# Splitting queries and keys once per head pair, with SBUF transfers and a block-diagonal product for the last queries

## The chip, the cores and the metric

The kernel runs on one core of one Trainium2 chip. The metric is device time in microseconds of that core, as the median over runs; less is better. The engines are named as the profile names them: PE (TensorE), DVE (VectorE), ACT (ScalarE), POOL (GpSimd), SP (SyncE, which issues most of the DMAs).

## What is computed

Attention with a threshold over 8 batches, 8 heads, 576 positions and 64 dimensions per head, and then a mixing layer of width 512 on each batch's result. All in fp32.

```python
scores = scale * np.matmul(q, k.transpose(0, 1, 3, 2))
thresh = np.max(scores, axis=-1, keepdims=True) - tau
scores = np.where(scores >= thresh, scores, -1000000000.0)
attn = np.exp(scores - np.max(scores, axis=-1, keepdims=True))
attn = attn / (np.sum(attn, axis=-1, keepdims=True) + 1e-09)
x = np.matmul(attn, v)            # heads side by side: [B, 576, 512]

theta = x @ w_theta
zr, zi = x * np.cos(theta), x * np.sin(theta)
y = np.einsum('ts,bsd->btd', w_tok_r, zr) + np.einsum('ts,bsd->btd', w_tok_i, zi)
u = x + y
out = u + np.maximum(u @ w_ch, 0.0)
```

## The kernel before

**Tiling.** A head pair (two of the eight heads of a batch) is the unit of attention; there are 32 pairs. The 576 queries of a head are four blocks of 128 and a last one of 64. Units 0 to 3 of a pair are the full blocks, each done for head 0 and then for head 1 ("half units", written (i, j)); unit 4 is the last 64 queries of both heads at once. So a pair has nine half units, in the order 0, 1, 2, 3, 4.

**Products.** To keep fp32 precision, operands are split into a high part (a cast to fp32r) and the rest. For a score, the stationary operand `qq` holds the high part of 64 dimensions on partitions 0 to 63 and the rest of the same dimensions on partitions 64 to 127; the moving operands are `k1` (high part, on both halves) and `k2` (rest). That is why `load_raw` (L213) loads each head's [64 x 576] twice, into both halves of a 128-partition tile: four 144 KB loads for a pair's queries and four for its keys. Per head ACT scales the queries (L225) and casts them (L226), POOL subtracts (L228); for keys ACT casts and POOL subtracts (`split`, L100 and L109). A full half unit is four matmuls of 288 columns (L278). Unit 4 needs both heads' keys: ten matmuls, since head 1's columns are stored rotated by 64 and its second half wraps round.

**After a score.** DVE negates it and takes the maximum (L282), ACT takes the Exp (L299), DVE masks and sums (L300). PE then transposes the result (`flip`, L326; ACT copies it, L331), and multiplies with the values (`values`, L361). At a pair's end `invert` and `normalize` divide by the sums.

**The mixing layer.** When a batch's four pairs are done its mixing layer (`moe`) is cut into pieces that `fill` puts on PE between the half units of the next batch: the angle product (L402), the sines and cosines on ACT (L463, L464, with z their result), their transposes (L487; cast zh on ACT L489, rest zl on DVE L490), the token product (L504) and the channel product (L402 again). An activation table must be loaded for Sin and again for Exp; `after` sets an order only, here the table load (L459) behind DVE's absolute value of the angle.

**Order.** PE's order is written out by hand (`manual_schedule`): at each step the score of the half unit three steps ahead (`AHEAD`), then a fill, then the flip of the present one, and another fill. On the other engines a scheduler sets the order by priority. Loads are requested at fixed half units of the pair before: queries at (0, 0), keys at (1, 0), values at unit 4. Raw tiles share a pool of four buffers (`t576`) with the angle work; key tiles have six buffers, four a pair. In the first batch the weights are also loaded and decoded from a wide format, mostly on DVE.

Of the kernel before, what the change touches and what calls it, by code (L numbers as in the profile page):

```python
# [10 lines left out]
F32 = mybir.dt.float32  # L11
# [28 lines left out]
def tile_attn_moe(  # L40
# [11 lines left out]
    nc = tc.nc  # L52
    B, NP, D, _, S = qT.shape
# [60 lines left out]
    def after(ins, other):  # L114

        info = mybir.DependencyInfo(mybir.DependencyClass.NoSync, mybir.DependencyReason.DATA)
        tc.add_manual_dep(ins.ins, other.ins.name, info, reason="order")
        return ins
# [76 lines left out]
    qq_t = []  # L195
    for i in range(2):
        qq = const.tile([P, S + SP], F32R, name=f"qq{i}")
        nc.gpsimd.memset(qq[:, S:SP].bitcast(F32), 0.0)
        qq_t.append(qq)
# [10 lines left out]
    def load_raw(n, src, name, j):  # L210
# [5 lines left out]
    def prepare_q(n, heads=(0, 1)):  # L216

        if 0 in heads:
            pairs[n] = SimpleNamespace(n=n, b=n // NP, p=n % NP, keys=[], a={})
        pr = pairs[n]  # L220
        pr.qf = qq_t[n % 2]
        for j in heads:
            raw = load_raw(n, qT, f"qraw{n}", j)
            qq = pr.qf[:, SP * j : SP * j + S]
            nc.scalar.activation(out=raw, in_=raw, func=AF.Copy, scale=gate)  # L225
            nc.scalar.copy(out=qq, in_=raw)  # L226
            eng = nc.gpsimd if n else nc.vector
            eng.tensor_tensor(out=qq[64:128], in0=raw[64:128], in1=qq[64:128].bitcast(F32), op=ALU.subtract)  # L228

    def prepare_k(n, j):  # L230

        pr = pairs[n]
        raw = load_raw(n, kT, f"kraw{n}", j)
        k1 = pool.tile([P, S], F32R, tag="k", name=f"k1_{n}_{j}", bufs=6)
        k2 = pool.tile([P, S], F32R, tag="k", name=f"k2_{n}_{j}", bufs=6)
        split(nc.scalar, nc.gpsimd if n else nc.vector, k1, k2, raw)
        pr.keys.append((k1, k2))
# [11 lines left out]
    def new_unit(n, i):  # L249
        pr = pairs[n]  # L250
        if i == 0:
# [7 lines left out]
    def score(u, j):  # L259
# [3 lines left out]
        if u.i < 4:  # L263
            c = u.i * P + (0 if j == 0 else SP + 64)
            parts = [(pr.qf[:, c : c + P], j, kk, 0) for kk in pr.keys[j]]
        else:
            parts = [(pr.qf[:, 512:SP], 0, kk, 0) for kk in pr.keys[0]]
# [424 lines left out]
```

## Time and profile before

| what | us |
|---|---|
| median of 3 runs | 1160.27 |
| fastest and slowest of them | 1159.11, 1160.57 |
| span of the profiled execution | 1161.3 |

The profile shows one execution. Busy shares of the whole span mix three parts: some 130 us in which the first batch's attention goes with the decoding of the weights, seven periods of about 133 us with one batch's attention and the batch before's mixing layer, and the last batch's mixing layer alone. So a stretch is read by itself before a line of it is. In a timeline a line gives the start, the time, the line of code, the operation, and in brackets how long its engine stood idle before it and what released it. PE's matmuls are pipelined, so the distance between two starts, not the duration, is what they take.

### The profile page before, as it was taken

What the parts mean: (1) busy time and instruction counts of PE and PEld (TensorE: products, weight loads), DVE (VectorE), ACT (ScalarE), POOL (GpSimd) and SP (SyncE); (2) the same over time, 40 slices, a digit from 0 to 9 for tenths busy, and PEclk for the clock granted to TensorE, in tenths of its full rate; (3) what the DMA queues carried; (4) which work ended last, traced back from release to release, by engine and by line L of the source; (5) the groups of instructions that cost most, each with busy time, mean ns of one, the idle gap of its engine ahead of it and who ended that gap; (6) DMA issues with size and microseconds to landing.
All of it is one profiled execution on the core that took longest, in us unless ns stands there. A gap on an engine that the chain in (4) does not pass through costs nothing.

```text
span 1161.3 us, 21157 instructions
## 1 busy us (share of the span) xinstructions
PE 1054.1 (91%) x7736; PEld 923.7 (80%) x7736; DVE 833.7 (72%) x2107; ACT 764.4 (66%) x1434; POOL 369.1 (32%) x295
## 2 busy tenths in 40 slices
PE   4987888889989999899999999899989998899998
PEld 3565686778878888798878888788878988788898
DVE  7998876986767677765877667675877667676462
ACT  6656868655696667964697657865688655965350
POOL 2203125231352233522344233422335312530110
PEclk9989999989999999999999999999999999999999
DMA  7722222343332152212432142312432133310411
GB/s 254 203 84 77 63 71 62 118 141 99 108 96 62 32 165 86 80 42 77 129 115 63 31 137 84 100 52 60 144 86 83 42 101 101 98 32 1 127 60 60
DMA packets 55176, 105.26 MB, mean 91 GB/s; under 512 B 11936, under 2 KB 20128, under 8 KB 55072
## 3 DMA queue, kind: packets, MB, share of 16 engines
q1 hardware_dynamic: 45856, 70.35, 20.3%
q0 software_dynamic: 9216, 33.56, 10.1%
q8 instruction: 61, 1.00, 0.4%
q14 instruction: 43, 0.35, 0.1%
HBM read 90.24 MB, written 13.63 MB: 89 GB/s over the span
## 4 chain that ended last, share of the span: by engine, by line
PE 54%; ACT 18%; DVE 17%; DMA 5%; issue 5%; SPq 1%; ACTq 0%; DVEq 0%
PE y_ps L504 13%; PE m_ps L402 11%; PE s_ps L278 10%; PE o_ps L361 9%; PE t_ps L326 6%; DVE s_sb L300 4%; DVE sc L282 4%; ACT s_sb L299 3%; DMA qraw<-in_qT_dram 3%; ACT z L463 2%; DMA out_dram<-xT 2%; ACT L459 2%; ACT a L331 2%; ACT L468 2%; DVE th L446 2%
## 5 line engine op out<-in xcount | busy, mean ns | idle before, releaser
L300 DVE SCALAR_TENSOR_TENSOR s_sb<-sc,nm,s_sb 128x576 f32<-128x576 f32 x288 | 274.2, 952 | 107.2 <-ACT s_sb L299 103.0
L278 PE MATMUL s_ps<-k,qq 128*128 128x288 f32 (+1 forms) x1344 | 243.7, 309 | 61.6 <-DVE sc L282 41.2
L299 ACT ACTIVATE s_sb<-sc,nm 128x576 f32<-128x576 f32 x288 | 223.7, 779 | 105.7 <-DVE sc L282 104.8
L282 DVE TENSOR_SCALAR_CACHE_REDUCE sc<-s_ps 128x576 f32<-128x576 f32 x288 | 216.7, 752 | 80.9 <-PE s_ps L278 78.1
L278 PEld LDWEIGHTS s_ps<-k,qq 128*128 128x128 f32 x1344 | 194.5, 193 | 94.3 <-DVE sc L282 52.4
L331 ACT COPY a<-t_ps 128x512 f32<-128x512 f32 x256 | 148.4, 580 | 51.8 <-PE t_ps L326 51.1
L326 PE MATMUL t_ps<-ident,s_sb 128*128 128x128 f32 x1152 | 176.6, 276 | 5.3 <-DVE zl L490 5.0
L361 PE MATMUL o_ps<-a,v 128*64 128x320 f32 (+1 forms) x1280 | 170.2, 412 | 3.5 <-DVE xT L507 3.5
L504 PE MATMUL y_ps<-wt_h,zh 128*128 128x288 f32 x576 | 166.4, 307 | 4.6 <-ACT zh L489 3.8
L504 PE MATMUL y_ps<-wt_l,zh 128*128 128x288 f32 x576 | 164.2, 303 | 0.0
L326 PEld LDWEIGHTS t_ps<-ident,s_sb 128*128 128x128 f32 x1152 | 142.0, 142 | 10.2 <-DVE zl L490 7.1
L228 POOL TENSOR_TENSOR qq<-qraw,qq 64x576 fp32r<-64x576 f32 x62 | 101.8, 1642 | 140.5 <-ACT qq L226 85.9
L361 PEld LDWEIGHTS o_ps<-a,v 128*64 128x64 f32 x1280 | 88.8, 137 | 64.0 <-issue 7.2
L109 POOL TENSOR_TENSOR k<-kraw,k 128x576 fp32r<-128x576 f32 x62 | 90.9, 1466 | 145.4 <-ACT k L100 144.5
L192 POOL DMA_DIRECT2D wm<-wm_dram x64 | 36.5, 570 | 265.7 <-PE m_ps L402 234.0
L504 PEld LDWEIGHTS y_ps<-wt_h,zh 128*128 128x128 f32 x576 | 109.2, 190 | 6.7 <-ACT zh L489 4.4
L504 PEld LDWEIGHTS y_ps<-wt_l,zh 128*128 128x128 f32 x576 | 109.4, 190 | 0.0
L504 PE MATMUL y_ps<-wt_h,zl 128*128 128x288 f32 x576 | 103.5, 305 | 0.0
L402 PE MATMUL m_ps<-xh,wm 128*128 128x288 f32 x512 | 91.1, 307 | 8.8 <-ACT th L440 8.4
L402 PE MATMUL m_ps<-uh,wm 128*128 128x288 f32 x512 | 85.0, 301 | 11.9 <-ACT uh L100 11.9
L475 POOL TENSOR_TENSOR z<-z,xT 128x576 f32<-128x576 f32 x56 | 79.5, 1442 | 32.7 <-ACT z L463 22.9
L109 POOL TENSOR_TENSOR ul<-xT,uh 128x576 fp32r<-128x576 f32 x24 | 34.7, 1446 | 169.4 <-DVE uh L104 121.4
(85 smaller groups left out, 1608.5 us busy)
## 6 DMA issues: line engine op xcount, KB each, us to landing
wm<-wm_dram POOLq DMA_DIRECT2D x64, 512.0 KB, 4.2
qraw<-in_qT_dram SPq DMA_DIRECT2D x128, 144.0 KB, 3.0
kraw<-in_kT_dram SPq DMA_DIRECT2D x128, 144.0 KB, 2.9
out_dram<-xT SPq DMA_DIRECT2D x32, 288.0 KB, 4.3
v<-in_vp_dram SPq DMA_DIRECT2D x32, 256.0 KB, 2.8
wraw<-in_w_tok_dram SPq DMA_DIRECT2D x9, 576.0 KB, 4.7
wraw<-in_w_theta_dram SPq DMA_DIRECT2D x4, 512.0 KB, 5.4
wm_dram<-whi SPq DMA_DIRECT2D x8, 256.0 KB, 2.3
```

Source lines behind the costliest of these rows:

```text
L109: eng_lo.tensor_tensor(out=lo, in0=src, in1=hi.bitcast(F32), op=ALU.subtract)
L228: eng.tensor_tensor(out=qq[64:128], in0=raw[64:128], in1=qq[64:128].bitcast(F32), op=ALU.subtract)
L278: nc.tensor.matmul(ps[:, h, d0:d1], st, kk, start=(x == 0), stop=(x == len(todo) - 1))
L282: nc.vector.tensor_scalar(out=sc.rearrange("p (a b) -> p a b", a=2), in0=ps[:, :, :HS], scalar1=-1.0, scalar2=None, op0=ALU.mult, op1=ALU.min,
L299: nc.scalar.activation(out=e, in_=u.ps[j], func=AF.Exp, bias=nm[:, j : j + 1], scale=-1.0)
L300: nc.vector.scalar_tensor_tensor(out=e, in0=u.ps[j], scalar=nm[:, 2 + j : 3 + j], in1=e, op0=ALU.is_le, op1=ALU.mult, accum_out=u.pr.rows[ ...
L326: nc.tensor.transpose(out=tp[:, c * P : (c + 1) * P], in_=u.sf[:, k0 + c * P : k0 + (c + 1) * P], identity=ident)
L331: nc.scalar.copy(out=t.a[:, :, j, q0 : q0 + P], in_=tp.rearrange("p (c q) -> p c q", c=4))
L361: nc.tensor.matmul(o[64 * j : 64 * j + 64, :w], st, mv, start=(c == 0), stop=(c == 4))
L402: nc.tensor.matmul(tiles[h][:, :HS], wm[:, a, c, :], parts[c][bb][:, hs], start=(count[h] == 0), stop=(count[h] == 11))
L475: lo_eng.tensor_tensor(out=zi, in0=zi, in1=x, op=ALU.mult)
L504: nc.tensor.matmul(ps[:, :HS], z, w, start=(n == 0), stop=(n == len(work) - 1))
```

## The change

The layout of queries and keys changes, and with it the order of the units.

- `load_raw` loads a pair's raw queries in one transfer of 128 partitions (head 0 on 0 to 63, head 1 on 64 to 127), and its keys in another. They are scaled, cast and subtracted once for both heads.
- New transfers within SBUF (`move`, on SP's queue) then build what the products need: `qq` (high part and rest of one head, four moves of 64 x 512), the key tiles (each head's part on both halves of the partitions, in `spread_k`: four moves for head 0, eight for head 1, whose columns are turned by 64 on the way), and `tails`.
- `tails` are two 128 x 128 tiles with the last 64 queries of head 0 in one corner and of head 1 in the other, zeros elsewhere. With the split keys of both heads, `kk`, as they are, unit 4 is three products of two halves: six matmuls.
- Unit 4 comes first in a pair; groups, sums and the token weights' rows and columns are reordered to match, and the output is put back by the host.
- Key tiles have four buffers (one pair) where they had six. Queries for the next pair are requested at unit 4, keys at (0, 1), the key moves at (2, 0) and (2, 1).
- The Sin table load now waits on DVE's absolute value.

```diff
     def load_raw(n, src, name):
         raw = temp(name)
-        for r in (slice(0, 64), slice(64, P)):
-            nc.sync.dma_start(raw[r], src[n // NP, n % NP, :, j])
+        nc.sync.dma_start(raw, src[n // NP, n % NP].rearrange("j d s -> (j d) s"))
         return raw
...
+    def prepare_q(n):
+        pr = pairs[n] = SimpleNamespace(n=n, b=n // NP, p=n % NP, keys=[], a={}, tails=tails)
+        raw = load_raw(n, qT, f"qraw{n}")
+        hi = temp(f"qh{n}", F32R)
+        lo = raw.bitcast(F32R)
+        nc.scalar.activation(out=raw, in_=raw, func=AF.Copy, scale=gate)
+        nc.scalar.copy(out=hi, in_=raw)
+        eng = nc.gpsimd if n else nc.vector
+        eng.tensor_tensor(out=lo, in0=raw, in1=hi.bitcast(F32), op=ALU.subtract)
+        for t, x in zip(tails, (hi, lo)):
+            for j in range(2):
+                r = slice(64 * j, 64 * j + 64)
+                move(t[r, r], x[r, 512:])
+        pr.qq = []
+        for j in range(2):
+            qq = pool.tile([P, 512], F32R, tag="qq", name=f"qq{n}_{j}", bufs=4)
+            for x, y in ((0, hi), (64, lo)):
+                move(qq[x : x + 64], y[64 * j : 64 * j + 64, :512])
+            pr.qq.append(qq)
...
+    def spread_k(n, j):
+        pr = pairs[n]
+        for x in range(2):
+            t = pool.tile([P, S], F32R, tag="k", name=f"k{x}_{n}_{j}", bufs=4)
+            src = pr.kk[x][64 * j : 64 * j + 64]
+            for r in (slice(0, 64), slice(64, P)):
+                if j == 0:
+                    move(t[r], src)
+                else:
+                    move(t[r, 64:], src[:, :512])
+                    move(t[r, :64], src[:, 512:])
+            pr.keys.append(t)
...
         else:
-            parts = [(pr.qf[:, 512:SP], 0, kk, 0) for kk in pr.keys[0]]
-            parts += [(pr.qf[:, S : S + P], 1, kk, 64) for kk in pr.keys[1]]
+            (qh, ql), (kh, kl) = pr.tails, pr.kk
+            parts = [(qh, kh), (qh, kl), (ql, kh)]
...
-            ahead_of = after(nc.scalar.preload_act_table(AF.Sin), ab)
+            ahead_of = after(nc.scalar.preload_act_table(AF.Sin), ab, wait=True)
...
-    halfs = [(n, i, j) for n in range(B * NP) for i in range(5) for j in range(2 if i < 4 else 1)]
+    halfs = [(n, i, j) for n in range(B * NP) for i in (4, 0, 1, 2, 3) for j in range(2 if i < 4 else 1)]
...
             if n + 1 < B * NP:
-                if (i, j) == (0, 0):
+                if i == 4:
                     prepare_q(n + 1)
-                if (i, j) == (1, 0):
-                    for jj in range(2):
-                        prepare_k(n + 1, jj)
-                if i == 4:
+                if (i, j) == (0, 1):
+                    prepare_k(n + 1)
+                if (i, j) == (1, 1):
                     load_v(n + 1)
+                if i == 2:
+                    spread_k(n + 1, j)
```

On PE, pair 16's unit 4 (a row is the line, the operation, its output and inputs, and the shape; `k1_16_j` and `k2_16_j` are the high part and the rest of head j's keys). Before:

```order
L278 MATMUL s_ps_6654<-k1_16_0_6148,qq0_83 128x288
L278 MATMUL s_ps_6654<-k2_16_0_6149,qq0_83 128x288
L278 MATMUL s_ps_6654<-k1_16_1_6155,qq0_83 128x288
L278 MATMUL s_ps_6654<-k2_16_1_6156,qq0_83 128x288
L278 MATMUL s_ps_6654<-k1_16_0_6148,qq0_83 128x288
L278 MATMUL s_ps_6654<-k2_16_0_6149,qq0_83 128x288
L278 MATMUL s_ps_6654<-k1_16_1_6155,qq0_83 128x224
L278 MATMUL s_ps_6654<-k1_16_1_6155,qq0_83 128x64
L278 MATMUL s_ps_6654<-k2_16_1_6156,qq0_83 128x224
L278 MATMUL s_ps_6654<-k2_16_1_6156,qq0_83 128x64
```

The same unit, now at the pair's start, where `kh16` and `kl16` are both heads' split keys and `tail_h`, `tail_l` the block-diagonal queries:

```order
L293 MATMUL s_ps_6436<-kh16_6292,tail_h_83 128x288
L293 MATMUL s_ps_6436<-kl16_6293,tail_h_83 128x288
L293 MATMUL s_ps_6436<-kh16_6292,tail_l_85 128x288
L293 MATMUL s_ps_6436<-kh16_6292,tail_h_83 128x288
L293 MATMUL s_ps_6436<-kl16_6293,tail_h_83 128x288
L293 MATMUL s_ps_6436<-kh16_6292,tail_l_85 128x288
```

Ten matmuls became six of 288 columns, on tiles that no key move writes.

On ACT, a block of sines beside pair 14, before (L299 is the Exp, L331 and L344 flip copies, L489 the cast zh):

```order
L459 ACT_TABLE_LOAD
L463 ACTIVATE z_5311<-z_5311,small_74 128x576
L464 ACTIVATE z_5311<-th_5090 128x576
L464 ACTIVATE z_5313<-th_5166 128x576
L331 COPY a0_5197<-t_ps_5382 128x4x128
L344 COPY a50_5198<-t5_ps_5388 128x128
L299 ACT_TABLE_LOAD
L299 ACTIVATE s_sb_5364<-sc_5371,nm_5365 128x576
L463 ACT_TABLE_LOAD
L463 ACTIVATE z_5313<-z_5313,small_74 128x576
L468 ACT_TABLE_LOAD
L489 CAST zh_5410<-z_ps_5412 128x128
```

The same block after:

```order
L316 ACTIVATE s_sb_5513<-sc_5520,nm_5514 128x576
L476 ACT_TABLE_LOAD
L480 ACTIVATE z_5437<-z_5437,small_74 128x576
L481 ACTIVATE z_5437<-th_5207 128x576
L480 ACTIVATE z_5439<-z_5439,small_74 128x576
L481 ACTIVATE z_5439<-th_5288 128x576
L485 ACT_TABLE_LOAD
L316 ACTIVATE s_sb_5513<-sc_5560,nm_5514 128x576
```

The four sines stand together, and the two loads around an Exp between them are gone; this is so in the seven blocks that had them.

On SP, the program's start, before (the number in `qraw0`, `kraw0` is the pair):

```order
L80 DMA small_74<-in_tau_dram 128x1
L213 DMA qraw0_93<-in_qT_dram 64x576 x2
L213 DMA kraw0_99<-in_kT_dram 64x576 x2
L213 DMA qraw0_106<-in_qT_dram 64x576 x2
L213 DMA kraw0_112<-in_kT_dram 64x576 x2
L132 DMA wraw_171<-in_w_theta_dram 128x1024
```

And after:

```order
L80 DMA small_74<-in_tau_dram 128x1
L216 DMA qraw0_93<-in_qT_dram 128x576
L133 DMA wraw_205<-in_w_theta_dram 128x1024
L133 DMA wraw_187<-in_w_theta_dram 128x1024
L133 DMA wraw_320<-in_w_theta_dram 128x1024
L133 DMA wraw_300<-in_w_theta_dram 128x1024
L133 DMA wraw_450<-in_w_tok_dram 128x1152
L216 DMA kraw0_109<-in_kT_dram 128x576
L216 DMA qraw1_209<-in_qT_dram 128x576
L212 DMA tail_h_83<-qh0_95 64x64 x2
L212 DMA tail_l_85<-qraw0_93 64x64 x2
L212 DMA qq0_0_103<-qh0_95 64x512
```

Five weight loads moved ahead of the first pair's keys and of its moves; two more (of `w_tok`) stand between those of the queries and those of the keys.

On SP, the key moves of pair 22 after, a third pair of its batch (`kh22`, `kl22` are the split keys, `k0_22_j` and `k1_22_j` the tiles of head j):

```order
L216 DMA kraw22_8847<-in_kT_dram 128x576
L212 DMA k0_22_0_8979<-kh22_8849 64x576 x2
L212 DMA k1_22_0_8982<-kl22_8850 64x576 x2
L212 DMA k0_22_1_9021<-kh22_8849 64x512
L212 DMA k0_22_1_9021<-kh22_8849 64x64
L212 DMA k0_22_1_9021<-kh22_8849 64x512
L212 DMA k0_22_1_9021<-kh22_8849 64x64
L212 DMA k1_22_1_9026<-kl22_8850 64x512
```

Twelve new transfers follow the load in the queue, of which the four for head 0 come first; before there were none.

## Rows read from the trace of the kernel before

**Rows 1.** The page's first part: busy us, share of the span, instructions.

```profile
PE 1054.1 (91%) x7736; PEld 923.7 (80%) x7736; DVE 833.7 (72%) x2107; ACT 764.4 (66%) x1434; POOL 369.1 (32%) x295
```

**Rows 2.** Three stretches: length, busy us by engine, clock, DMA share, GB/s.

```profile
0.00:30.00 30.00, 13.32 (x42) 10.02 (x43) 21.36 (x51) 18.53 (x28) 6.53 (x14) 1.00 0.80 256
30.00:100.00 70.00, 60.65 (x324) 42.95 (x322) 67.81 (x160) 45.89 (x92) 15.53 (x11) 0.93 0.46 131
681.00:815.00 134.00, 125.25 (x956) 111.60 (x957) 95.28 (x251) 92.96 (x175) 48.30 (x37) 1.00 0.30 85
```

**Rows 3.** PE's timeline near 706 us: start, us, line, in brackets idle time before.

```profile
706.32 1.42 PE L278 MATMUL s_ps<-k,qq 128*128 128x288 f32 x10
707.57 0.78 PE L402 MATMUL m_ps<-xh,wm 128*128 128x288 f32 x4
...
709.80 0.69 PE L278 MATMUL s_ps<-k,qq 128*128 128x288 f32 x4
710.33 0.69 PE L402 MATMUL m_ps<-xh,wm 128*128 128x288 f32 x4
```

**Rows 4.** PE's timeline, waits on ACT, DVE and POOL from 730 to 751.

```profile
730.77 0.66 PE L326 MATMUL t_ps<-ident,s_sb 128*128 128x128 f32 x4 [0.92 <-DVE zl L490]
...
733.15 0.80 PE L278 MATMUL s_ps<-k,qq 128*128 128x288 f32 x4 [0.49 <-DVE sc L282]
...
745.47 0.63 PE L487 MATMUL z_ps<-ident,z 128*128 128x128 f32 x4 [0.79 <-DVE zl L490]
...
747.11 0.67 PE L278 MATMUL s_ps<-k,qq 128*128 128x288 f32 x3 [0.48 <-POOL k L109]
...
750.51 0.78 PE L278 MATMUL s_ps<-k,qq 128*128 128x288 f32 x4 [0.70 <-DVE rows L366]
```

**Rows 5.** ACT's timeline around raw queries and sines, same batch.

```profile
728.74 0.78 ACT L225 ACTIVATE qraw<-qraw,small 128x576 f32<-128x576 f32 x1 [3.06 <-DMA qraw<-in_qT_dram]
...
739.26 1.28 ACT L299 ACT_TABLE_LOAD   x1
...
741.35 1.28 ACT L463 ACT_TABLE_LOAD   x1
...
743.44 1.28 ACT L468 ACT_TABLE_LOAD   x1
744.73 0.27 ACT L489 CAST zh<-z_ps 128x128 fp32r<-128x128 f32 x1
```

**Rows 6.** Groups by line and form: count, busy us, mean ns, idle before.

```profile
L300 DVE SCALAR_TENSOR_TENSOR s_sb<-sc,nm,s_sb 128x576 f32<-128x576 f32 x288 | 274.2, 952 | 107.2 <-ACT s_sb L299 103.0
...
L225 ACT ACTIVATE qraw<-qraw,small 128x576 f32<-128x576 f32 x64 | 49.8, 779 | 24.9 <-DMA qraw<-in_qT_dram 21.8 <-DVE sc L282 3.0
L100 ACT CAST k<-kraw 128x576 fp32r<-128x576 f32 x64 | 43.2, 675 | 29.1 <-PE s_ps L278 26.9 <-DMA kraw<-in_kT_dram 2.0
L226 ACT CAST qq<-qraw 128x576 fp32r<-128x576 f32 x64 | 43.2, 675 | 0.5
```

**Rows 7.** DVE's and POOL's timelines, same batch.

```profile
747.64 1.42 POOL L109 TENSOR_TENSOR k<-kraw,k 128x576 fp32r<-128x576 f32 x1 [0.59 <-ACT k L100]
...
748.28 1.40 DVE L300 SCALAR_TENSOR_TENSOR s_sb<-sc,nm,s_sb 128x576 f32<-128x576 f32 x1 [0.59 <-ACT s_sb L299]
```

**Rows 8.** DMA issues: count, KB each, median us from issue to landing.

```profile
qraw<-in_qT_dram SPq DMA_DIRECT2D x128, 144.0 KB, 3.0
...
out_dram<-xT SPq DMA_DIRECT2D x32, 288.0 KB, 4.3
...
wraw<-in_w_theta_dram SPq DMA_DIRECT2D x4, 512.0 KB, 5.4
```

**Rows 9.** SP's queue: one issue of two half loads; SP's waits by releaser.

```profile
726.93 1.19 SPq L213 DMA_DIRECT2D qraw<-in_qT_dram  x2
...
SPq L213 <- DVE th L446: 217.8, 14, 29.7
```

**Rows 10.** PE's timeline, the first score.

```profile
8.58 1.79 PE L278 MATMUL s_ps<-k,qq 128*128 128x288 f32 x4 [8.58 <-DVE qq L228]
```

More of the change, by code (lines that the diff above doesn't have):

```diff
@@ L112, in temp, with after @@
         return pool.tile([P, S], dt, tag="t576", name=name, bufs=4)
-    def after(ins, other):
-        info = mybir.DependencyInfo(mybir.DependencyClass.NoSync, mybir.DependencyReason.DATA)
+    def after(ins, other, wait=False):
+        kind = mybir.DependencyClass.Sync if wait else mybir.DependencyClass.NoSync
+        info = mybir.DependencyInfo(kind, mybir.DependencyReason.DATA)
         tc.add_manual_dep(ins.ins, other.ins.name, info, reason="order")
@@ L193, in get_wm @@
         return t
[L195 to L199, printed above, removed]
+    tails = []
+    for x in ("h", "l"):
+        t = const.tile([P, P], F32R, name="tail_" + x)
+        nc.gpsimd.memset(t.bitcast(F32), 0.0)
+        tails.append(t)
     v5_t = []
@@ L208, in tile_attn_moe, with move, load_raw @@
     pairs = {}
-    def load_raw(n, src, name, j):
+    def move(out, in_):
+        nc.sync.dma_start(out.bitcast(F32), in_.bitcast(F32))
+    def load_raw(n, src, name):
         raw = temp(name)
-        for r in (slice(0, 64), slice(64, P)):
-            nc.sync.dma_start(raw[r], src[n // NP, n % NP, :, j])
-        return raw
-    def prepare_q(n, heads=(0, 1)):
-        if 0 in heads:
-            pairs[n] = SimpleNamespace(n=n, b=n // NP, p=n % NP, keys=[], a={})
-        pr = pairs[n]
[L221 to L228, printed above, removed]
@@ new lines, in prepare_k @@
+    def prepare_k(n):
+        pr = pairs[n]
+        raw = load_raw(n, kT, f"kraw{n}")
+        pr.kk = [pool.tile([P, S], F32R, tag="kk", name=f"{x}{n}", bufs=2) for x in ("kh", "kl")]
+        split(nc.scalar, nc.gpsimd if n else nc.vector, *pr.kk, raw)
+    def spread_k(n, j):
+        pr = pairs[n]
+        for x in range(2):
[8 more added lines that the diff above has]
+            pr.keys.append(t)
@@ L347, in flip_last @@
                 r = slice(64 * j, 64 * j + 64)
-                nc.scalar.copy(out=t.a5[r, 256:320], in_=tp[r, r])
+                nc.scalar.copy(out=t.a5[r, :64], in_=tp[r, r])
     def values(pr, g):
@@ L361, in values @@
                 nc.tensor.matmul(o[64 * j : 64 * j + 64, :w], st, mv, start=(c == 0), stop=(c == 4))
[L362 removed]
+        nc.scalar.copy(out=xT[pr.n][:, 320 * g : 320 * g + w], in_=o[:, :w])
     def invert(pr):
@@ L665 @@
     last = vv[:, :, :, 512:].reshape(B, H // 2, 128, 1, D)
-    wr = _np.asarray(inputs["moe_w_tok_r"]).T
-    wi = _np.asarray(inputs["moe_w_tok_i"]).T
+    wr = _np.asarray(inputs["moe_w_tok_r"]).T[order][:, order]
+    wi = _np.asarray(inputs["moe_w_tok_i"]).T[order][:, order]
     feeds = {
@@ L690 @@
     got = r.results[0]["out_0_dram"]
-    return _np.ascontiguousarray(got.transpose(0, 2, 1))
+    out = _np.empty((B, S, H * D), got.dtype)
+    out[:, order] = got.transpose(0, 2, 1)
+    return out
```

58 lines of the change are left out of this document (23 added, 35 removed).

## The prediction

> **What bounds the kernel now.** I read the page's busy shares first: PE is busy for 91% of the span, DVE for 72%, ACT for 66% [rows 1]. That is a mean, so next I read the stretches [rows 2]. From 30 to 100 us DVE is the engine without room (67.81 of 70 us: the weights are decoded there beside batch 0's attention), and PE runs at a clock of 0.93. In a later batch, 681 to 815 us, PE has 125.25 of 134 us at clock 1.00, and DVE 95.28, ACT 92.96 and POOL 48.30. So in seven of the eight batches the time is PE's own work plus the 134.00 − 125.25 = 8.75 us in which PE, whose instructions run in a fixed order, waits for an input. Anything taken from ACT, POOL or the DMA queues counts only if one of those waits ends on it. The reader is to see in PE's own rows which waits these are [rows 4].
>
> **PE's own work.** A pair's ten-matmul unit is at 706.32 and the next line starts at 707.57: 1.25 us. An ordinary unit's four matmuls take 710.33 − 709.80 = 0.53 us, 0.133 each [rows 3]. Six cost 0.80, so a pair gains 0.45 us. It counts in the 28 pairs of batches 1 to 7; in batch 0 DVE hides it. 28 × 0.45 = **−12.6 us**. This term is sure, unless PE waits for the product's inputs: the block-diagonal queries and the keys of both heads. These need only the load, the split and the 16 KB moves, and are issued more than half a pair ahead.
>
> **ACT and POOL.** Two heads' scaling and two casts become one of each on 128 partitions: ACT loses 32 × (779 + 675 + 675) ns = 68 us [rows 6]. In ACT's order the 14 sine tables that are loaded again inside a block go too, 14 × 1.28 = 18 us [rows 5]. Of 764 us that is 11%, but off PE's path; it is worth what it takes from PE's 8.75 us. I looked behind each wait:
> - 730.77 (0.92 us) and 733.15 (0.49): ACT had just been given the two heads' raw queries, late (3.06 us of waiting, then 0.78 and 0.67 us of work for each head [rows 5, 6]); the cast zh and the Exp that PE waited for stood behind them. One of two sets remains: half, 0.70 us.
> - 745.47 (0.79): the cast zh at 744.73 stood behind the loads at 739.26, 741.35 and 743.44. Two of the three go, 2.6 us: all of it.
> - 747.11 (0.48) and 750.51 (0.70): the first waits for POOL's subtraction for a key tile. The second stands behind a DVE mask that took 1.40 us beside the next one on POOL [rows 7]; its kind takes 0.95 on the mean [rows 6]. In the changed order the key split comes a turn and a half earlier, once: all of it, 1.18.
>
> Together 0.70 + 0.79 + 1.18 = 2.67 us a batch; 7 × 2.67 = **−18.7 us**. The low end is nothing (another wait ends just behind), the high one all five, 3.38 × 7 = −23.7. The rest of the 8.75 us isn't touched and stays.
>
> **The added wait.** The sine table's load now waits for DVE's absolute value, with Exps, flip copies and zh casts queued behind it on ACT, and PE behind those. The sine itself needed that value already, and the rows show no idle time there but a block in pieces [rows 5]. Scores run three half units ahead, so I cost it at nothing; if that cover is gone, it gives back the 0.79 of 745.47, which is inside the bounds above.
>
> **The moves.** SP's queue gets 20 moves a pair and loses 6 loads of 8. At 0.60 us an issue [rows 9] 25 issues are 15 of a pair's 33 us, so SP isn't full. What matters is when the last key move lands. Keys now have buffers for one pair only, so head 1's eight moves can't start before the last score of the pair has read the old keys, and must land before the next pair's (0, 1) score. By the rows of the changed order and 0.133 us a matmul, PE has 9.0 us of work between those two points (9.0 to 9.4 in the four pairs of a batch); for head 0 it is about the same with half the moves. No SBUF-to-SBUF transfer stands in this trace. The nearest row for issuing one is a 64-partition load, 1.19 / 2 = 0.60 us [rows 9]; for landing, the 144 KB load, 3.0 us, and at the bad end the slowest load, 5.4 [rows 8]. Eight issues and one landing behind the 0.53 us of the last score: 0.53 + 4.8 + 3.0 = 8.3, inside 9.0 by 0.7 us. I take 3.0, since the bytes and partitions are those of that row. Once a batch an output of 288 KB stands in the same queue; with its landing, 4.3, the sum is 9.6, 0.6 us late: 7 × 0.6 = **+4 us**. Third pairs have a longer chain: their raw load waits for a buffer that DVE's angle work frees, a wait SP has 14 times, up to 29.7 us [rows 9]; raw queries, split, moves and raw keys then follow one another. That leaves 0 to 4 us late each batch, so the ends of this term are 0 and +28.
>
> The Trainium skill speaks against this part: "DMA: Bandwidth & Descriptors", section Rules for kernel authors, says that two transfers to disjoint partition halves serialize and that one 128-partition transfer should be used. By it head 1's moves wouldn't overlap, and the last could land as at the bad end above. No run here shows two such moves; this trace's pairs of half loads do land at 3.0 us.
>
> **The start.** Before, the first score runs at 8.58 us [rows 10]. Now one load of queries is followed on SP by five weight loads, 2.6 MB, before the first moves. At the 256 GB/s of the first 30 us [rows 2], 3.2 MB take 12.6 us, and a landing of 3.0 puts the first score at 15 to 16: 7 us late. The per-head keys come behind two more weight loads, so the upper end is twice that, +14. Against this stand DVE's 30.00 − 21.36 = 8.6 idle us [rows 2]: weights that come sooner can be decoded there, and what isn't left for 30 to 100 us is won back; half of it, −4, is the low end. I take **+5 us**, the middle.
>
> **The sum.** Against the profiled execution, 1161.3: −12.6 − 18.7 + 4 + 5 = −22.3, so 1139.0. The median of the runs lies 1.0 below the span: **1138**.
>
> **Rivals.** *Keys late in every pair.* If moves land like the slowest load, 0.53 + 4.8 + 5.4 = 10.7 us against 9.0: 1.7 us of PE waiting at (0, 1), 28 × 1.7 = 48 us. 1161.3 − 12.6 − 18.7 + 5 + 48 − 1.0 = **1182**, slower. It decides from 26.3 / 28 = 0.94 us a pair, that is when head 1's last move lands more than 9.9 us after the previous pair's last score. For it: eight serial issues, and a buffer for one pair only. Against it: 0.7 us of margin at this trace's own landings, and DMA busy 30% of a batch. Chance 0.18.
>
> *ACT and POOL were cover only.* The PE waits stay, each ending on the next thing: 1161.3 − 12.6 + 4 + 5 − 1.0 = **1157**. For it: the wait at 750.51 stands only 3.4 us behind the one at 747.11, so one that goes may leave the next. Against it: 86 us gone from ACT, spread over all batches. Chance 0.13.
>
> *The start costs all of +14:* 1138 + 9 = **1147**. For it: eight loads ahead of the key moves. Against it: DVE's idle time. Chance 0.10.
>
> The forecast with its own spread, 1121 to 1150, has the other 0.59.
>
> **The numbers.** The range reaches below to all five waits gone and the best start, 1161.3 − 12.6 − 23.7 − 4 − 1.0 = 1120; I put 1119. Above, it takes in the late start and the covered ACT; of the first rival it takes the mild third (the third pairs alone, +28 in place of +4, give 1162), and ends at 1166. Left out are about 0.14 above and 0.04 below. A measurement of this kernel tells 0.2% from no change, here 1158.0 to 1162.6. Faster: the forecast 0.58, the late start 0.10, half of the covered case 0.07, together 0.75. Same: the other half and a mild lateness, 0.08. Slower: 0.17.
>
> **What would show it.** Score units of six matmuls near 0.80 us; no table load inside a sine block; ACT about 86 us less busy; no PE wait of the kinds at 730.77, 745.47 and 747.11. The first score at about 15 us, and the second batch's first Exp no more than 5 us later than before. A PE wait at the (0, 0) or (0, 1) score that ends on a key move, in most pairs and of a microsecond or more, would make the forecast wrong; in third pairs alone it would cost what I allowed. So would a first batch longer by over 14 us.

## The result and the profile after

The changed kernel takes 1149.63 us (median of 4 runs, 1148.71 to 1151.60), the kernel before 1160.42 beside it; the ratio is 0.9889, interval 0.9866 to 0.9911. The forecast of 1138 had the way right and double the size: 10.8 us were gained, not 22. Two more measurements beside the kernel before, on other chips, gave 0.9942 (0.9924 to 0.9960) and 0.9916 (0.9889 to 0.9943). The mean of the three is 0.9916, about 10 us, and chips differ by more than one interval; so below a run is set against the kernel before measured beside it on the same chip. Where the changed kernel wasn't measured beside it too, the comparison with that kernel is uncertain by the spread of these three, some 3 us either way.

The profiled execution spans 1146.9 us, 14.4 less than before. The page's first part shows that all engines have less to do [rows 1]:

```profile
PE 1033.3 (90%) x7608; PEld 907.0 (79%) x7608; DVE 821.2 (72%) x2105; ACT 682.8 (60%) x1324; POOL 271.2 (24%) x233
```

ACT lost 81.6 us where I had counted 86, POOL 98. The groups by line and form show how: half as many scalings and casts at the same price as before [rows 6], and 16 table loads each way, none inside a block.

```profile
L225 ACT ACTIVATE qraw<-qraw,small 128x576 f32<-128x576 f32 x32 | 24.9, 779 | 29.1 <-DMA qraw<-in_qT_dram 28.0 <-issue 1.0
L100 ACT CAST kh<-kraw 128x576 fp32r<-128x576 f32 x32 | 21.8, 682 | 13.8 <-DMA kraw<-in_kT_dram 13.7
L226 ACT CAST qh<-qraw 128x576 fp32r<-128x576 f32 x32 | 21.7, 678 | 0.8 <-DVE kl L109 0.8
L476 ACT ACT_TABLE_LOAD x16 | 20.5, 1283 | 6.1 <-DVE z L472 6.0
L485 ACT ACT_TABLE_LOAD x16 | 20.5, 1283 | 0.3
```

On PE's timeline a pair's first unit now runs from 703.41 to 704.31, where its ten matmuls took 1.25 us [rows 3]:

```profile
703.41 0.40 PE L293 MATMUL s_ps<-kh,tail_h 128*128 128x288 f32 x1
703.65 0.30 PE L293 MATMUL s_ps<-kl,tail_h 128*128 128x288 f32 x1
...
704.18 0.29 PE L293 MATMUL s_ps<-kh,tail_l 128*128 128x288 f32 x1
704.31 0.70 PE L419 MATMUL m_ps<-xh,wm 128*128 128x288 f32 x4
```

That is 0.90 us, 0.10 more than six times 0.133, since the first of them takes 0.24. The units of the other pairs take 0.89 to 0.91. A pair gains 0.35 us, 28 pairs 9.8.

**Where the time went.** The first Exp of each batch, read from ACT's timeline, cuts the span into stretches (us). Batches are counted from 0; "b1" and "b2 to b6" are the time from a batch's first Exp to the next one's, and "rest" is the last batch with its mixing layer:

| kernel | first Exp | first Exp of b1 | b1 | b2 to b6 | rest | span |
|---|---|---|---|---|---|---|
| before | 11.2 | 138.3 | 143.3 | 667.0 | 212.7 | 1161.3 |
| after | 19.2 | 139.9 | 136.5 | 661.4 | 209.1 | 1146.9 |
| after, second measurement | 19.1 | 139.4 | 141.7 | 663.2 | 209.8 | 1154.1 |
| after, third | 19.5 | 141.1 | 137.1 | 662.2 | 209.7 | 1150.1 |

The five steady batches gain only 4 to 6 us, about 1 a batch, where PE's own work alone should give 4 × 0.35 = 1.4 and the waits 2.7 more. Batch 1, which was 10 us longer than the steady ones before, gains 2 to 7 us by itself, and the rest 3 to 4.

So new waits stand where old ones went. The list of PE's waits over the five steady batches (us in total, times, the longest) has, before:

```profile
PE s_ps L278 <- DVE sc L282: 11.3, 11, 1.6
PE m_ps L402 <- ACT th L440: 6.0, 5, 1.2
```

and after:

```profile
PE s_ps L293 <- DVE sc L299: 22.2, 24, 2.2
PE z_ps L504 <- ACT th L457: 10.2, 5, 2.0
```

The kinds at 730.77, 745.47, 747.11 and 750.51 [rows 4] made up 10.4 us before, and none of them is left. But PE stands idle for 42.5 us of these batches (43.8 and 42.9 in the other two profiles), and it was 41.0 before. PE's timeline and the clock of four stretches show the longest wait that comes in every batch, behind the sines:

```profile
583.49 0.91 PE L504 MATMUL z_ps<-ident,z 128*128 128x128 f32 x4 [2.04 <-ACT th L457]
584.54 1.33 PE L419 MATMUL m_ps<-xh,wm 128*128 128x288 f32 x4
585.80 3.01 PE L378 MATMUL o_ps<-a,v 128*64 128x256 f32 x20
```

```profile
581.00:583.40 2.40, 0.45 (x5) 0.21 (x2) 0.02 (x1) 2.37 (x5) 2.40 (x3) 1.00 0.17 60
583.40:586.00 2.60, 2.37 (x10) 1.72 (x12) 2.56 (x2) 2.59 (x7) 2.24 (x2) 0.56 0.00 0
586.00:588.00 2.00, 2.00 (x16) 1.13 (x16) 2.00 (x5) 0.99 (x3) 0.00 (x0) 0.72 0.30 83
588.00:590.00 2.00, 2.00 (x19) 1.54 (x16) 0.71 (x3) 0.84 (x2) 0.00 (x0) 1.00 0.46 134
```

PE stands for 2.04 us behind ACT's eviction of the angle. In the stretch that begins with its return the granted clock is 0.56, near the lower level (1.2 GHz), and four matmuls that else take 0.78 take 1.33. From 588 on it is 1.00 again. ACT's timeline shows why the eviction was late:

```profile
577.74 1.28 ACT L476 ACT_TABLE_LOAD   x1 [0.67 <-DVE z L472]
...
581.64 1.28 ACT L485 ACT_TABLE_LOAD   x1
582.94 0.41 ACT L457 ACTIVATE th<-m_ps 128x288 f32<-128x288 f32 x1
```

The table load waits 0.67 us for DVE's absolute value: the added wait. Then load, four sines and load hold ACT until 582.94. A batch has two blocks of sines; this is the first, which was in one piece before too.

The second kind, on DVE's and PE's timelines while the queries of a third pair are being moved:

```profile
599.89 0.46 DVE L462 TENSOR_SCALAR km<-th 128x576 f32<-128x576 f32 x1 [2.51 <-DMA qq<-qh]
...
601.06 0.75 DVE L299 TENSOR_SCALAR_CACHE_REDUCE sc<-s_ps 128x576 f32<-128x576 f32 x1
...
601.87 0.81 PE L293 MATMUL s_ps<-k,qq 128*128 128x288 f32 x4 [1.84 <-DVE sc L299]
```

DVE's angle step takes a tile of the shared pool that the query moves still read. It stands 2.51 us, the copy of the scores (L299) behind it, and PE behind that. This happens once in each of six batches, 7.1 us in all on DVE. Each time the move that DVE waited for had landed 3.1 to 5.2 us after its issue, with a 512 KB weight tile (`wm`) issued shortly before it; half of all such moves land in 2.4 or less. A third kind is the raw query load behind twelve key moves in SP's queue:

```profile
808.47 0.78 ACT L225 ACTIVATE qraw<-qraw,small 128x576 f32<-128x576 f32 x1 [2.55 <-DMA qraw<-in_qT_dram]
```

An Exp stands behind it, and the next score on PE:

```profile
813.23 0.80 PE L293 MATMUL s_ps<-k,qq 128*128 128x288 f32 x4 [2.18 <-DVE sc L299]
```

What didn't happen is key tiles coming late pair after pair. Outside the first 30 us one score waits on one, at some 248 us, for 1.0 us (3.9 and 1.3 in the other two profiles). The page's list of DMA issues gives the median landing of head 0's key moves:

```profile
k<-kh SPq DMA_DIRECT2D x64, 144.0 KB, 2.5
k<-kl SPq DMA_DIRECT2D x64, 144.0 KB, 2.7
```

### The profile page after: what moved, and what is told of

It is laid out like the page before. It is cut to its first block, busy times and chain, and to the rows that moved or that the text cites. A ratio compares the mean times of both kernels' runs of the same rounds, so it can differ in the third digit from the quotient of the medians.

```text
span 1146.9 us, 21522 instructions
## 1 busy us (share of the span) xinstructions
PE 1033.3 (90%) x7608; PEld 907.0 (79%) x7608; DVE 821.2 (72%) x2105; ACT 682.8 (60%) x1324; POOL 271.2 (24%) x233
## 4 chain that ended last, share of the span: by engine, by line
PE 49%; DVE 15%; ACT 15%; DMA 9%; SPq 6%; issue 5%; ACTq 0%; DVEq 0%
PE y_ps L521 13%; PE s_ps L293 9%; PE o_ps L378 8%; PE m_ps L419 8%; SPq L212 6%; PE t_ps L343 5%; DVE s_sb L317 4%; DMA qraw<-in_qT_dram 3%; DVE sc L299 3%; ACT s_sb L316 3%; DMA kraw<-in_kT_dram 2%; ACT z L480 2%; DMA qq<-qraw 2%; DVE xl L109 2%; ACT L476 2%
## 5 line engine op out<-in xcount | busy, mean ns | idle before, releaser
L317 DVE SCALAR_TENSOR_TENSOR s_sb<-sc,nm,s_sb 128x576 f32<-128x576 f32 x288 | 264.2, 917 | 79.4 <-ACT s_sb L316 74.4
L299 DVE TENSOR_SCALAR_CACHE_REDUCE sc<-s_ps 128x576 f32<-128x576 f32 x288 | 216.6, 752 | 113.9 <-PE s_ps L293 111.4
L293 PE MATMUL s_ps<-k,qq 128*128 128x288 f32 x1024 | 195.1, 313 | 56.4 <-DVE sc L299 48.5
L293 PEld LDWEIGHTS s_ps<-k,qq 128*128 128x128 f32 x1024 | 151.9, 193 | 73.9 <-DVE sc L299 63.6
L378 PE MATMUL o_ps<-a,v 128*64 128x256 f32 (+1 forms) x1280 | 175.9, 422 | 1.1 <-ACT a L350 1.0
L228 POOL TENSOR_TENSOR qraw<-qraw,qh 128x576 fp32r<-128x576 f32 x31 | 44.3, 1429 | 212.7 <-ACT qh L226 206.8
L492 POOL TENSOR_TENSOR z<-z,xT 128x576 f32<-128x576 f32 x56 | 82.8, 1508 | 29.4 <-ACT z L480 29.4
L521 PEld LDWEIGHTS y_ps<-wt_h,zl 128*128 128x128 f32 x576 | 83.5, 189 | 0.0
L419 PEld LDWEIGHTS m_ps<-uh,wm 128*128 128x128 f32 x512 | 72.0, 188 | 13.8 <-ACT uh L100 13.3
```

The source lines that it names most:

```text
L228: eng.tensor_tensor(out=lo, in0=raw, in1=hi.bitcast(F32), op=ALU.subtract)
L293: nc.tensor.matmul(ps[:, h, :HS], st, kk[:, h * HS : (h + 1) * HS], start=(x == 0), stop=(x == len(parts) - 1))
L299: nc.vector.tensor_scalar(out=sc.rearrange("p (a b) -> p a b", a=2), in0=ps[:, :, :HS], scalar1=-1.0, scalar2=None, op0=ALU.mult, op1=ALU.min,
L317: nc.vector.scalar_tensor_tensor(out=e, in0=u.ps[j], scalar=nm[:, 2 + j : 3 + j], in1=e, op0=ALU.is_le, op1=ALU.mult, accum_out=u.pr.rows[ ...
L378: nc.tensor.matmul(o[64 * j : 64 * j + 64, :w], st, mv, start=(c == 0), stop=(c == 4))
L419: nc.tensor.matmul(tiles[h][:, :HS], wm[:, a, c, :], parts[c][bb][:, hs], start=(count[h] == 0), stop=(count[h] == 11))
```

## The experiments

The sections give the ratio to the kernel before, measured beside it, and its interval. "Lost to the clock" is, over windows of 2 us, the sum of PE's busy time × (1 − granted clock), in batches 2 to 6; the kernel before has 0.0 there, the changed kernel 6.3, 6.5 and 6.6 in its three profiles.

### Four matmuls back in

```diff
-            parts = [(qh, kh), (qh, kl), (ql, kh)]
+            parts = [(qh, kh), (qh, kl), (ql, kh), (qh, kl), (ql, kh)]
```

> The changed kernel, with ten matmuls of 288 columns in the first unit of a pair in place of six (two products are added a second time, so the last queries' scores are other numbers; the work around them is the same). Theory (the matmuls taken out are worth their own time in seven batches): 28 x 4 x 0.133 = 15 us longer, 1164 to 1165. Rival (PE's order has slack at that place, so matmuls there cost little): under 7 us longer, below 1157.

Ratio 1.0047 (1.0022 to 1.0072), median 1168.1: against the mean of the changed kernel, 0.9916, that is 0.0131, 15 us longer (12 to 18 against its three measurements), as the first theory says. Batches 2 to 6 take 671.2 us, 9 more than the changed kernel, where 20 × 4 × 0.133 is 10.6. PE's order has no slack at that place; the term for PE's own work stands. These ten matmuls are not those of the kernel before: all have 288 columns, and the unit takes 1.43 us where the old ten took 1.25, so the run puts back more (0.53 us a pair) than the change took out (0.35).

### Lighter ACT and POOL without the moves

The kernel before, with head 1 on head 0's operands from the second pair on:

```diff
-        for j in heads:
+        for j in heads if n == 0 else (0,):
...
+        if j == 1 and n > 0:
+            pr.keys.append(pr.keys[0])
+            return
...
-            c = u.i * P + (0 if j == 0 else SP + 64)
+            c = u.i * P + (0 if j == 0 or pr.n else SP + 64)
...
-            parts += [(pr.qf[:, S : S + P], 1, kk, 64) for kk in pr.keys[1]]
+            last = pr.qf[:, 512:SP] if pr.n else pr.qf[:, S : S + P]
+            parts += [(last, 1, kk, 64) for kk in pr.keys[1]]
```

> The kernel before, in which from the second pair on head 1 takes head 0's queries and keys (its results are head 0's scores with head 1's values; head 1's queries and keys are neither loaded nor split). PE's instructions are the same in number and shape; ACT is relieved of 66 us and POOL of some 96 us, as by the change, without any move and without the six-matmul unit. Recorded sum: the waits behind queries and keys go, 0.70 + 1.18 us in seven batches, 13 us shorter, 1147 where the kernel before has 1160 (ratio 0.989). Theory now (a PE wait that goes lets the next one in): under 5 us shorter, ratio 0.996 or more.

Ratio 0.9813 (0.9787 to 0.9838), median 1142.45 against 1164.26: 22 us, more than the recorded sum and four times what my theory after the result allowed. That theory falls: waits of PE that go behind queries and keys do shorten the run. The page's first part shows PE's instructions unchanged in number [rows 1] and ACT and POOL relieved about as in the changed kernel:

```profile
PE 1043.0 (91%) x7736; PEld 913.6 (80%) x7736; DVE 832.1 (73%) x2107; ACT 706.3 (62%) x1341; POOL 278.3 (24%) x233
```

The gain lies all along: the first Exp of batch 1 at 133.7 (before 138.3), batch 1 140.0, batches 2 to 6 659.7, the rest 208.2. So the relief helps the first batch too, which I had not counted: 4.6 us. The loads of head 1 are gone here as well, 4 of 8 a pair, and so are half the takers of raw tiles and of the six key buffers, so the 22 us hold whatever those cost; the run doesn't separate it.

### The waiting table load alone, and both together

```diff
-            ahead_of = after(nc.scalar.preload_act_table(AF.Sin), ab)
+            ahead_of = after(nc.scalar.preload_act_table(AF.Sin), ab, wait=True)
```

in the kernel before, and in the light kernel above (with `after` taught to wait, as in the changed kernel).

> The kernel before with the one edit that the Sin table load waits on DVE's absolute value; 14 table loads go from ACT. Recorded sum: 0.79 us in seven batches, 5 to 6 us shorter (ratio 0.995). Theory now (the block of sines in one piece holds PE for 2 us, and some batches then run 4 us at the lower clock): no gain, ratio 0.999 to 1.006, with granted clocks under 1 behind that wait in several of the batches 2 to 6, where the kernel before has none.

> Both at once: the kernel before with head 1 on head 0's queries and keys (results as in the first run of this call) and the waiting table load; all that the change takes from ACT and POOL, and nothing else of it. Recorded sum: 19 us shorter, ratio 0.984. Theory now: under 7 us shorter, ratio 0.994 or more.

Alone: ratio 1.0036 (1.0019 to 1.0053), 4 us slower. In the light kernel: 0.9855 (0.9831 to 0.9878), 5 us more than without. The wait costs, in both. In the kernel before with the wait, PE's timeline and the clock of two stretches read:

```profile
594.86 0.79 PE L403 MATMUL m_ps<-xh,wm 128*128 128x288 f32 x4 [1.37 <-ACT th L441]
595.58 4.60 PE L362 MATMUL o_ps<-a,v 128*64 128x320 f32 x20
```

```profile
596.00:598.00 2.00, 2.00 (x12) 0.89 (x10) 2.00 (x2) 1.98 (x4) 1.09 (x1) 0.51 0.00 0
598.00:600.00 2.00, 2.00 (x12) 0.76 (x8) 2.00 (x6) 0.48 (x2) 0.00 (x0) 0.64 0.39 93
```

In the kernel before, the same wait is 1.21 us, the clock behind it stays at 1.00, and the same twenty value matmuls take 2.91 us:

```profile
721.53 0.81 PE L402 MATMUL m_ps<-xh,wm 128*128 128x288 f32 x4 [1.21 <-ACT th L440]
722.27 2.91 PE L361 MATMUL o_ps<-a,v 128*64 128x320 f32 x20
```

PE's wait for this eviction is only 0.16 us longer than in the kernel before. The larger new wait stands behind the second block of sines, the one that the added wait makes one piece. On POOL's and PE's timelines:

```profile
611.97 5.56 POOL L476 TENSOR_TENSOR z<-z,xT 128x576 f32<-128x576 f32 x4 [3.23 <-issue]
617.49 3.81 POOL L109 TENSOR_TENSOR k<-kraw,k 128x576 fp32r<-128x576 f32 x2
...
619.47 0.72 PE L279 MATMUL s_ps<-k,qq 128*128 128x288 f32 x3 [1.92 <-POOL k L109]
```

The four sines come in a row, POOL's four operations on them too, and both key subtractions stand behind these. Over batches 2 to 6 PE waits 9.8 us for POOL's key tiles, where it was 1.9. Lost to the clock in these batches: 12.7 us, three stretches behind the eviction, three behind POOL's key tiles and one with another wait, of 2.98 us. The five batches take 671.4, 4.4 more. Without that loss they would be 658.7, 8 us under the kernel before, if none of the lost time was covered by other waits. So taking the loads out of the block may bring what I had counted or more, and POOL's late subtraction and the clock take more than that back. In the light kernel POOL has half the subtractions, and PE never waits for a key tile there. For both together the recorded sum (19 us, 0.984) lies inside the interval; my theory's 0.994 doesn't.

The reverse edit, in the changed kernel:

> The changed kernel, with the Sin table load ordered behind DVE's absolute value but not waiting on it, as before; the 14 loads inside the sine blocks come back. Theory (the sine blocks in one piece cost a wait of 2.0 us and some 0.5 to 2 us of slow PE clock behind it in each batch, 0.7 of it by the added wait): 0 to 7 us shorter than the changed kernel, 1143 to 1150. Rival (the recorded sum: the loads cost 0.79 us a batch of PE's time, and nothing speaks against taking them out): 5 to 6 us longer, 1155.

Ratio 0.9916 (0.9893 to 0.9940), the mean of the changed kernel's three measurements, none of which stood beside this one. On PE's timeline the wait behind the sines is 0.65 us shorter, and the twenty value matmuls behind it run at full clock:

```profile
584.66 0.63 PE L504 MATMUL z_ps<-ident,z 128*128 128x128 f32 x4 [1.39 <-ACT th L457]
585.71 0.79 PE L419 MATMUL m_ps<-xh,wm 128*128 128x288 f32 x4 [0.42 <-ACT a L348]
586.43 2.38 PE L378 MATMUL o_ps<-a,v 128*64 128x256 f32 x20
```

Nothing is lost to the clock in batches 2 to 6, and yet they take 667.3 us, no less than before: smaller waits stand in other places (0.69, 0.62 and 1.07 us at scores between 593 and 613). In the changed kernel no price of the wait is to be seen.

### Tiles of their own for the queries

```diff
-        raw = load_raw(n, qT, f"qraw{n}")
-        hi = temp(f"qh{n}", F32R)
+        raw = pool.tile([P, S], F32, tag="qraw", name=f"qraw{n}", bufs=1)
+        nc.sync.dma_start(raw, qT[n // NP, n % NP].rearrange("j d s -> (j d) s"))
+        hi = pool.tile([P, S], F32R, tag="qh", name=f"qh{n}", bufs=1)
```

> The changed kernel, with the raw queries and their high part in tiles of their own (one buffer each) and not in the shared pool of four. Theory (new waits took the place of the old): in the changed kernel DVE's angle step waits for moves that still read such a tile, 7.1 us in six batches, and the raw keys of a third pair come late for ACT, 11 us in the same batches; both go, each batch gets 1 to 2 us shorter, and the time is 6 to 12 us under the changed kernel's 1149.6: 1138 to 1144. Rival (PE's floor is reached, the next wait stands right behind): no more than 2 us less, 1147 to 1150.

Ratio 0.9979 (0.9947 to 1.0010), 4 to 10 us slower than the changed kernel; neither forecast held. DVE's waits on moves are gone, 0 where there were 6.6 us in batches 2 to 6; the time isn't. These batches take 664.0 us, and 11.2 are lost to the clock. PE's waits for the copy of the scores fell from 22.2 to 13.0 us, but 9.4 us of others came (for DVE's zl and ACT's flip copy) that the changed kernel hasn't. The profiled execution was the fastest of ten, 9 us under their median, so the trace doesn't show where the median's loss lies.

Then the same with the table load not waiting:

> The changed kernel with two edits: the raw queries and their high part in tiles of their own, and the Sin table load not waiting on DVE. Theory (of the gain of 22 us that the lighter ACT and POOL bring, some is lost to tiles that moves hold, and what the own tiles gave back in the first call was eaten by the lower clock behind the one-piece sine block): without that block both count, no slow-clock stretch in batches 2 to 6, and the time is 5 to 12 us under the changed kernel of this call. Rival (the loss is not in held tiles; late raw loads and the key chain remain, whatever holds them): within 3 us of the changed kernel of this call.

Ratio 0.9984 (0.9967 to 1.0001): also slower than the changed kernel (0.9916 beside it), and neither forecast held. Freeing the tiles brought nothing that can be seen; since new waits came with it, that doesn't show what the held tiles cost. Lost to the clock 7.3 us, three stretches of it with a wait of 2.47 us for DVE's zl, so the waiting table load isn't the only thing that lowers the clock. The first Exp of batch 1 came at 148.1, 8 us later than in the changed kernel; why I did not find. The scheduler's order on ACT and DVE is another one in both kernels.

### The first pair's keys ahead of the weights

```diff
         raw = load_raw(n, qT, f"qraw{n}")
+        if n == 0:
+            pr.kraw = load_raw(0, kT, "kraw0")
...
-        raw = load_raw(n, kT, f"kraw{n}")
+        raw = pr.kraw if n == 0 else load_raw(n, kT, f"kraw{n}")
```

> The changed kernel, with the first pair's keys loaded right behind its queries, and its key moves ahead of the later weight loads. Theory (DVE's decoding sets the first 130 us, the late first score is made up there): the first Exp comes 4 to 8 us earlier, the end no more than 3 us, 1147 to 1150. Rival (the late start is passed on): 5 to 8 us shorter, 1142 to 1145.

Ratio 0.9902 (0.9873 to 0.9932): within the changed kernel's three. The first Exp is 1.5 us earlier (17.7), the second batch's comes at 140.5. The edit moved the load, but most of the key moves still issue behind those of the queries, from 15 us on, and the start moved less than meant; so it bounds little; what can be said is that 1.5 us at the front weren't seen again at 140.

### The moves without anybody waiting for them

The light kernel, with 20 transfers a pair from a weight tile to two spare tiles, requested at the change's places:

```diff
+                if n >= 4 and (i, j) == (0, 1):
+                    qmoves()
+                if n >= 4 and i == 2:
+                    moves(j)
```

> The kernel before with head 1 on head 0's queries and keys from the second pair on (as in the second call), and from the fifth pair on 20 transfers within SBUF a pair, of the change's sizes and at its places, from a weight tile to two spare tiles that nobody reads: the moves' traffic and their place in SP's queue, without anyone waiting for them. The light kernel without them had ratio 0.981. Theory (what the moves cost is waits of engines for tiles and late loads in the chain of one pair): under 4 us more, ratio 0.981 to 0.985. Rival (traffic and queue: slower landings and later loads for everybody): 8 us or more on top, ratio 0.988 or more.

Ratio 1.0140 (1.0093 to 1.0186): 38 us over the light kernel. By the number the rival wins. But the run isn't what it was meant to be: nobody waits for these transfers and their source is ready early, and they didn't stay at their places. The trace has the first of the 540 at 50.7 us, in batch 0, the last at 545.5, in batch 3, some 40 a pair, twice the change's density; from batch 4 (563.1) on there is none. Yet batches 4 to 6 are 9 us longer than in the light kernel, batches 2 and 3 11.

Where the transfers are, SP's and ACT's timelines show a raw load among them, and ACT behind the load:

```profile
473.67 1.18 SPq L236 DMA_DIRECT2D qraw<-in_qT_dram  x2
...
477.94 0.78 ACT L248 ACTIVATE qraw<-qraw,small 128x576 f32<-128x576 f32 x1 [3.93 <-DMA qraw<-in_qT_dram]
```

And in all five steady batches two subtractions stand in a row on DVE's timeline ahead of the copy of the scores, which stood between them in the light kernel. In batch 4, and PE's wait in batch 6:

```profile
577.88 3.24 DVE L109 TENSOR_TENSOR xl<-xT,xh 128x576 fp32r<-128x576 f32 x2
581.04 0.74 DVE L309 TENSOR_SCALAR_CACHE_REDUCE sc<-s_ps 128x576 f32<-128x576 f32 x1
...
849.99 0.80 PE L305 MATMUL s_ps<-k,qq 128*128 128x288 f32 x4 [3.42 <-DVE sc L309]
```

PE waits 3.42 us there, where the light kernel waits 1.55, and the clock falls behind it in four of the five (6.5 us lost). That is 5 × 1.87 + 6.5 = 16 of the 20 us by which these batches are longer (679.9 against 659.7). In three of them no transfer to a spare tile runs, so it is the scheduler's order, moved by the added instructions, and no price of a transfer. The first two batches are 14 us longer, with transfers and another order at once; what is whose there stays open. So the run shows that an order can cost 16 us, and not what the change's moves cost.

### Raw loads from another queue

```diff
-        nc.sync.dma_start(raw, src[n // NP, n % NP].rearrange("j d s -> (j d) s"))
+        (nc.gpsimd if n else nc.sync).dma_start(raw, src[n // NP, n % NP].rearrange("j d s -> (j d) s"))
```

> The changed kernel with the raw query and key loads issued by POOL, from the second pair on, and not by SP, whose queue keeps the moves, the values and the outputs. ACT's order stays nearly the same. Theory (the moves cost by standing ahead of the raw loads in one queue, and ACT, in order, stands at a raw tile with the Exp behind it): ACT's waits for raw tiles in batches 2 to 6 fall from 29 us to under 14, and the time is 5 to 10 us under the changed kernel: ratio 0.982 to 0.987 where the changed kernel had 0.989 to 0.994. Rival (traffic, or the chain from tile to tile, whichever queue issues): those waits stay above 20 us, ratio 0.989 to 0.996.

Ratio 1.0003 (0.9973 to 1.0034): the gain is gone, and neither forecast held. ACT's waits for raw tiles in batches 2 to 6 fell to 15.4 us, from 28.8 to 29.1 in the three profiles of the changed kernel; over the whole run they are

```profile
ACT qraw L225 <- DMA qraw<-in_qT_dram: 20.7, 8, 4.5
...
ACT kh L100 <- DMA kraw<-in_kT_dram: 8.3, 8, 1.5
```

in place of 28.0 and 13.7. But batches 2 to 6 take 663.4 us, no less, with 8.0 lost to the clock; and the first batch and the second are longer (first Exp of batch 1 at 144.9, its period 144.8). POOL now stands at loads whose tiles aren't free, 53.3 us behind query moves and 14.4 us once behind the decoding of the weights, with its subtractions and weight tiles queued behind it. Two of POOL's lines of waits:

```profile
POOL kraw L216 <- DMA qq<-qraw: 53.3, 9, 6.7
...
POOL kraw L216 <- DVE mag L140: 14.4, 1, 14.4
```

The loads' waits moved from ACT to POOL; the run doesn't show what late raw loads on ACT cost.

### The changed kernel again

> The changed kernel itself, on the same chip as the other runs of this call, so that they can be set beside it: ratio 0.989 as at first, within its interval of 0.002.

> The changed kernel, on the same chip as the other runs of this call, to set them beside it: ratio 0.989 to 0.994, as in the two measurements so far.

0.9942 and 0.9916, as above. The first is outside what I expected: the same kernel on another chip differs by 0.005. The second lies inside.

## Why the prediction was right or wrong

**PE's own work: right, the size somewhat too large.** Recorded −12.6; the unit takes 0.90 us and not 0.80, so −9.8, and four matmuls put back cost 15 us, their own time.

**The waits behind ACT and POOL: right in kind, and rather more.** Recorded −18.7, of it 13 behind queries and keys. The light kernel gains 22 us with the table loads still in place, some 5 of them in the first batch, which I had left out. In the changed kernel too, no PE wait of the kinds at 730.77, 745.47 and 747.11 is left in the steady batches.

**The added wait: wrong.** Recorded as nothing, "which is inside the bounds above". It costs 4 us in the kernel before and 5 in the light kernel. I had checked that an Exp behind it has cover; I had not asked what else stands behind it. In the kernel before that was above all POOL's key subtraction (9.8 us of PE waits in five batches in place of 1.9). In the changed kernel it is the eviction of the angle, for which PE waits 2.04 us, and 1.39 without the added wait; the clock fell behind it in four of the five steady batches of each of the three profiles. There the whole price isn't shown: without the wait the ratio stays inside the changed kernel's spread. Light and waiting together give −17 us: near the −18.7, by two errors of opposite sign, which is luck.

**The moves: the step that failed.** Recorded +4. With −9.8 and −17, a change of −10 leaves +17 for all else: the start, the moves and the order that came with them (15 of it in the stretches that follow). By stretches, against the light waiting kernel less PE's own gain: batch 1's first Exp at 139.4 to 141.1 against 135.4, 5 us, the size of the recorded term for the start; batches 2 to 6 662 against 661.4 − 7 = 654, **8 us**; batch 1 and the rest 2. The 8 is a remainder and not a measured price: without the added wait on either side it is 667.3 against 659.7 − 7, 15 us.

The mechanism that I priced, key tiles late, isn't there: the last of a pair's twelve key moves landed within 2.9 us of its issue in every pair of batches 2 to 6 (3.4 and 3.8 in the other two profiles), not in 5.4, and the margin held but for single pairs. What I left unpriced is what stands beside the moves: tiles of the shared pool that they hold while DVE wants them, and raw loads behind them in SP's queue, with ACT's in-order queue behind the load. I had named the serial chain of third pairs, and counted it for the key tiles only.

The trace shows these waits ending on PE. Followed back from releaser to releaser, 3.5 us of PE's 22.2 us of score waits in batches 2 to 6 end on a held tile and 6.2 on a raw query load (up to 5.5, and 5.0 to 6.2, over the three profiles); in the light waiting kernel it is 0 and 2.2. That difference, 7 to 9 us, has the size of the 8, but it is a reading of traces. What these waits are worth isn't settled: taking either away (tiles of their own, loads on POOL) removed the wait and left the time, since the order on ACT and DVE and the slow-clock stretches moved with it.

The rule that I weighed ("DMA: Bandwidth & Descriptors", Rules for kernel authors, in the Trainium skill: transfers to disjoint halves serialize) didn't decide. In a quiet pair (603.8 to 610.9) twelve half moves issued 0.5 to 0.7 us apart landed 1.8 to 2.5 us after their issue each, the last no later than the first, so several were under way at once. Beside an output or a weight tile single ones took up to 6.7 us.

**The start: its sign came, its price isn't separated.** Recorded +5, first score at about 15: it came at 13.96, and the next, which needs head 0's keys, at 22.71:

```profile
13.96 0.58 PE L293 MATMUL s_ps<-kh,tail_h 128*128 128x288 f32 x1 [13.96 <-DMA tail_h<-qh]
...
22.71 0.58 PE L293 MATMUL s_ps<-k,qq 128*128 128x288 f32 x1 [6.23 <-DMA k<-kh]
```

8 us at the first Exp were 1.1 to 2.8 at the second batch's, inside the 5 that I had set, or 5 beside a kernel with the same relief. That last figure compares two orders: in the runs that kept the change's start, the second batch's first Exp came anywhere from 139.4 to 148.1.

**Signs and range.** The first rival (1182) fell with its mechanism. The second, all cover (1157), fell with the light kernel; but what it foretold for PE, no less idle time, is what the steady batches show (41.0 us before, 42.5 to 43.8 after), by new waits and not by the next ones in line. The third, the late start (1147), stands 3 us from the first measurement and lacks its sign, a late second batch. The measured time lies between the forecast and the second rival, for reasons of neither.

**No version that beats both** came out. The lightest edits to the changed kernel, the table load not waiting and the earlier keys, lie inside its spread; the others are slower than it.

## What to carry to other kernels

Where PE waits on engines that run in order, relief of those engines can be worth what the waits at its end say, and was worth more here (22 us against 13); the way in which the relief is bought has to be priced in the same rows: which tile each new transfer holds, who takes that tile next, and what stands behind it in the queue. A wait that is added ahead of a long block on an engine must be followed to everything behind the block, and a PE wait of 1 to 2 us must be priced with the slow clock that may follow it. With a scheduler that orders by a model, an edit moves the order elsewhere too, and transfers that nobody waits for don't stay where they were written: the trace decides whether a run tested what it was made for.

## What the hardware showed

- After a wait of PE the granted clock often fell to its lower level (1.2 GHz): 0.56 and then 0.72 in the stretches from 583.4 to 588, and twenty value matmuls of 320 columns took 4.60 us in place of 2.91. Behind the angle's eviction, in batches 2 to 6, it fell after none of ten waits of 1.06 to 1.21 us (light kernel, kernel before), after 4 of 20 of 1.37 to 1.39 (the four kernels in which the wait has that length), and after 12 of 15 of 2.04 (the changed kernel's three profiles). It did so behind other waits as well, but not behind each: at 813.23 one of 2.18 us was followed by four score matmuls at full speed (0.80 us). Over batches 2 to 6 this cost up to 12.7 us of 671.
- A transfer of half the partitions within SBUF landed 2.3 to 2.5 us after its issue for 128 or 144 KB, and 1.7 to 2.0 for 16 KB, in quiet stretches; beside an output or a weight tile such transfers took 4 to 6.7 us.
- The same two kernels stood at 0.9889, 0.9942 and 0.9916 on three chips. Half a per cent between two kernels isn't settled by one chip.
